# When a load may wait for two neighbouring slots, and the order of three VectorE instructions in the last MLP

## The chip, the cores and the metric

The kernel runs on one core of one Trainium2 chip. The metric is the device time of one execution in microseconds; the median of several runs counts. The core has a TensorE (matmul; its weight loads are shown as PEld), a VectorE (DVE), a ScalarE (ACT), a GpSimd (POOL) and a SyncE (SP), which issues all of this kernel's transfers from HBM on one queue served by 16 DMA engines.

## The reference

Two identical layers follow each other; each is an attention over a cache and then a small MLP mixer, for 8 batch rows with one token each (D = 448).

```python
def _A_ref(x, k_cache, v_cache, wq, wo):
    q = (x @ wq).reshape(B, Sq, 16, 256).transpose(0, 2, 1, 3)
    k = jnp.repeat(k_cache, 2, axis=1)          # k_cache, v_cache: (8, 8, 4096, 256) bf16
    v = jnp.repeat(v_cache, 2, axis=1)
    scores = jnp.einsum("bhqd,bhkd->bhqk", q, k) * (256 ** -0.5)
    p = _softmax(scores, axis=-1)
    o = jnp.einsum("bhqk,bhkd->bhqd", p, v)
    return o.transpose(0, 2, 1, 3).reshape(B, Sq, 4096) @ wo
...
    x = x + _A_ref(_layernorm(x), A_k_cache, A_v_cache, A_wq, A_wo)
    x = x + _B_ref(_layernorm(x), B_w1, B_w2, B_w3, B_w4)
    x = x + _A_ref(_layernorm(x), A_k_cache, A_v_cache, A_wq, A_wo)
    x = x + _B_ref(_layernorm(x), B_w1, B_w2, B_w3, B_w4)
```

With one token the shifts of `_B_ref` leave zeros, so that B reduces to `x + gelu(layernorm(x) @ w3) @ w4`. The two caches are 134 MB each. Both layers read the same K and V, and nearly all of the traffic is theirs.

## The kernel before

**Units.** The work is a list of 144 places, called units. A unit is (layer, batch row, K/V head), that is one head over 4096 positions, or a GAP, which is empty. A unit has four quarters; a quarter needs one part of K and one of V, each 512 KB. For each batch row b the list has layer 1's heads, then a short stretch of GAPs and one or two stray heads in which the MLP of layer 1 and the query projection of layer 2 run (`mid_steps`), then layer 2's heads. `ends` holds the unit of layer 1's last head of each row (9, 27, 45, 63, 81, 98, 115, 132). `fence` holds the first unit of layer 2 of each row (14, 32, 50, 68, 85, 102, 119, 136); it can't start before the query is there. "The gap" below is what lies between an end and its fence. Batch rows, or batches, are counted from 0.

**Slots.** 31 slots of 512 KB (`slab`, N_SLOTS) hold everything that is loaded. K goes through VectorE first (`transposes`, L554), from its raw slot into another slot, and is read by TensorE (L645, `k_part`). V is read by TensorE as it landed (L622, `v_part`). Layer 1's transposed K of six of the eight heads stays in its slots until layer 2 has read it; one of these heads has two of its quarters parked in PSUM, and ScalarE copies them back (L512, 1.0 us a copy). A slot goes to the list `free` when its last reader has been written down in the program, and `pump` is called.

**pump** (L502) takes the next part from `loads` while more than RESERVE = 1 slots are free. All of this happens when the program is built: it fixes which transfer is issued where in SP's queue and into which slot. On the chip each transfer then waits for the last reader of its slot. A part with an even number, whose neighbour is in `wide` and close in the list, may be loaded with that neighbour in one transfer of 1 MB, if two neighbouring slots are free (`take_two`). If none are and `under_way`, the parts that are loaded and not yet read, is at least ENOUGH = 7, pump returns and nothing is issued until the next slot comes free. If fewer are under way, the part is loaded alone, into the first slot that has no free neighbour (`take`). `wide` holds the parts that are used in "calm" units: those from one past a fence to the next end. Parts of the gap are always loaded alone.

**A unit's work** on the engines: scores on TensorE (L645), maxima on DVE and TensorE (L660, L668, L678), exponentials on ScalarE (L681), a turn on TensorE (L704) and four casts on ScalarE (L712) that make the weights `pt` for V, the sum (L719) and its reciprocal on GpSimd (L723). About six quarters later come V's matmuls (L622), and two scalings on ScalarE (L591, `head_out`) write the head's result. `wo_mms` (L180) multiplies it by wo.

**The end.** After the last unit the second layer's MLP runs for all rows at once (L832 to L909). VectorE makes the gelu in four steps around ScalarE's tanh (L872, L875, L878, tanh L879, L884). GpSimd makes two powers (L867, `rr[:, 1]` first, then `rr[:, 0]`). L880 and L883 add the normalised residual, which needs `rr[:, 0]`. L884 makes `hT`, the operand of the 56 matmuls with w4 (L891), and L898 adds their results to the residual, one quarter of the columns at a time.

Of the kernel before, what the change touches and what calls it, by code (L numbers as in the profile page):

```python
# [11 lines left out]
ALU = mybir.AluOpType  # L12
# [11 lines left out]
LAG = 6  # L24
ENOUGH = 7
PAIR_VIEW = 12


@with_exitstack
def kernel(  # L30
# [14 lines left out]
    nc = tc.nc  # L45
# [345 lines left out]
    n_units = len(units)  # L391
# [11 lines left out]
    t = 0  # L403
    while t < n_units:
# [5 lines left out]
        n = 1  # L410
# [31 lines left out]
    for t in order:  # L442
        for s in range(4):
            i = late_v.get((t, s), 4 * t + s + LAG)
            if t in ends or units[t + 1 : t + 2] == [GAP]:
                i = 4 * t + (6, 6, 7, 7)[s]
            elif t + 1 == n_units:
                i = 4 * t + (5, 5, 6, 7)[s]
# [3 lines left out]
    loads = []  # L452
    wide = set()
    calm = [any(f < t for f in [-1] + list(fence) if not any(f < e < t for e in ends)) for t in range(n_units + 2)]
    k = 0
    for i in range(4 * n_units + 8):
        n = len(loads)
        while k < by[min(i, 4 * n_units - 1)]:
            loads.append(("k",) + parts[k])
            k += 1  # L460
        loads += [("v",) + p for p in plan.get(i, [])]
        if calm[min(i // 4, n_units)]:
            wide.update(loads[n:])
        t, q = divmod(i + 2, 4)
        if t < n_units and units[t] and units[t][0] == 2 and (units[t][2], q) in parked:
            loads.append(("p", t, q))
# [3 lines left out]
    under_way = [0]  # L470

    def take():

        lone = [x for x in free if x ^ 1 not in free]
        x = min(lone or free)
        free.remove(x)
        return x

    def take_two():

        both = [x for x in free if x % 2 == 0 and x + 1 in free]
        if both:
            free.remove(both[0])
            free.remove(both[0] + 1)
        return both[:1]
# [16 lines left out]
    def pump():  # L502
        while loads and len(free) > RESERVE:
            kind, t, i = loads[-1]
            _, b, g = units[t]
            if kind == "p":
                loads.pop()
                x = take()
                dst = slots[x].rearrange("p (e q c x) -> p q c e x", e=4, q=2, c=4)
                for j in range(2):  # L510
                    src = park[parked[g, i]][j][:].bitcast(BF16)
                    nc.scalar.copy(dst[:, j], src.rearrange("p (c e x) -> p c e x", c=4, e=4))  # L512
                kt_of[(1, b, g), i] = x
                continue
            cache, of = (A_k_cache, raw_of) if kind == "k" else (A_v_cache, v_of)
            n, two = 1, (kind, t, i + 1)
            if i % 2 == 0 and two in wide and two in loads[-PAIR_VIEW:]:
                x = take_two() if len(free) > RESERVE + 1 else []
                if x:
                    n, x = 2, x[0]  # L520
                    loads.remove(two)
                elif under_way[0] >= ENOUGH:
                    return
            loads.pop()
            if n == 1:
                x = take()
            src = cache[b, g].rearrange("(p s e) d -> p s (e d)", s=4, e=8)
            nc.sync.dma_start(
                slab[:, UNIT * x : UNIT * (x + n)].rearrange("p (s d) -> p s d", s=n),
                src[:, i : i + n],  # L530
            )
            for m in range(n):
                of[t, i + m] = x + m
            under_way[0] += n
            n_loads[0] += n
            if n_loads[0] >= 8 and extra:
                nc.sync.dma_start(*extra.pop(0))
# [3 lines left out]
    def transposes(i):  # L541


        while len(parts) - len(todo) < by[i]:
            t, s = todo[-1]
            if 4 * t + s > i and ((t, s) not in raw_of or not free):
                return
            todo.pop()
            raw = raw_of.pop((t, s))
            kt = kt_of[units[t], s] = take()  # L550
            src = slots[raw].bitcast(FP32).rearrange("p (q c e i) -> p q c e i", q=2, c=4, e=4)
            dst = slots[kt].bitcast(FP32).rearrange("p (e q c r) -> p q c e r", e=4, q=2, c=4)
            for q in range(2):
                nc.vector.transpose(dst[:, q], src[:, q])  # L554
            _, b, g = units[t]
            if (g, s) in parked:
                for q in range(2):
                    dst = park[parked[g, s]][q][:].rearrange("p (c e r) -> p c e r", c=4, e=4)
                    nc.vector.transpose(dst, src[:, q])
            free.append(raw)  # L560
            under_way[0] -= 1
            pump()
# [49 lines left out]
    def v_part(t, s):  # L612
        if s == 0:
            at = PO + 4 * (nth[t] % n_po)
            pos[t] = pyb[:, at : at + 4].rearrange("p (k h) -> p k h", h=2)
            if nth[t] == n_po // 2:
                nc.vector.memset(pyb[:, PO : PO + 4 * (len(order) - n_po)], 0.0)
        v = v_of.pop((t, s))
        vv = slots[v].rearrange("p (c d) -> p c d", d=Dh)
        for c in range(8):  # L620
            for k in range(2):
                nc.tensor.matmul(  # L622
                    pos[t][:, k, :],
                    vv[:, c, 128 * k : 128 * k + 128],
                    pts[t][:, 8 * s + c, :],
                    start=(t == 0 and s == 0 and c == 0 and k == 0),
                    stop=True,
                    skip_group_check=True,
                )
        free.append(v)  # L630
        under_way[0] -= 1
        pump()

    def k_part(t, s):
        u = units[t]
        p, b, g = u
        if s == 0:
            assert t not in runs or t in ready
            scs[t] = scb[t % 2][:, 0:64].rearrange("p (c b h) -> p c b h", b=4, h=2)
        key = (u if fresh(u, s) else (1, b, g)), s  # L640
        ktv = slots[kt_of[key]].rearrange("p (e c m x) -> p e c m x", e=4, c=2, x=2)
        for c in range(2):
            for db in range(4):
                for x in range(2):
                    nc.tensor.matmul(  # L645
                        scs[t][:, 2 * s + c, :, :],
                        ktv[:, db, c, :, x],
                        Qblk[run_of[t][0]][:, run_of[t][1], db, x, :, :],
                        start=(db == 0 and x == 0),
                        stop=(db == 3 and x == 1),  # L650
                    )
        if p == 2 or g in loose or (g, s) in parked:
            free.append(kt_of.pop(key))
            pump()
# [80 lines left out]
    for t in rowst:  # L735
# [10 lines left out]
        out=xc, in0=xf, scalar1=st[:, 1:2], scalar2=None, op0=ALU.add  # L746
# [6 lines left out]
        out=st[:, 3:4], in0=st[:, 2:3], in1=mhalf[0:Bn, 0:1], op=ALU.pow  # L753
# [30 lines left out]
    for t in range(n_units + 1):  # L784
        cur = t < n_units
        for q in range(4):
            i = 4 * t + q
# [50 lines left out]
    u, hh = fd[:, 128 : 128 + HC * Bn], fd[:, 256 : 256 + HC * Bn]  # L838
    hT = slots[3][:, 0 : HC * Bn]
# [10 lines left out]
        out=cu, in0=xb2, in1=mu.unsqueeze(2).to_broadcast([128, Bn, 4]), op=ALU.add  # L850
# [11 lines left out]
    for i in (1, 0):  # L862
        f, e = TWICE[i]
        nc.vector.tensor_scalar(
            out=tt[:, i], in0=va, scalar1=-f, scalar2=e, op0=ALU.mult, op1=ALU.add
        )
        nc.gpsimd.tensor_tensor(  # L867
            out=rr[:, i], in0=tt[:, i], in1=mhalf[:, 0:1].to_broadcast([128, Bn]), op=ALU.pow
# [4 lines left out]
        out=hv, in0=hp.rearrange("p (m b) -> p m b", b=Bn), in1=r1, op=ALU.mult  # L873
    )
    nc.vector.scalar_tensor_tensor(  # L875
        out=u, in0=hh, scalar=0.044715, in1=hh, op0=ALU.mult, op1=ALU.mult
    )
    nc.vector.scalar_tensor_tensor(out=u, in0=u, scalar=1.0, in1=hh, op0=ALU.add, op1=ALU.mult)  # L878
    nc.scalar.activation(u, u, ACT.Tanh, scale=0.7978845608028654)  # L879
    nc.vector.tensor_tensor(  # L880
        out=sq, in0=cu, in1=rr[:, 0].unsqueeze(2).to_broadcast([128, Bn, 4]), op=ALU.mult
    )
    nc.vector.tensor_tensor(out=xb2, in0=xb2, in1=sq, op=ALU.add)  # L883
    nc.vector.scalar_tensor_tensor(out=hT, in0=u, scalar=1.0, in1=hh, op0=ALU.add, op1=ALU.mult)  # L884
    xo = slots[5][:, 64 : 64 + 4 * Bn].rearrange("p (b c) -> p b c", c=4)
    xoc = xo.rearrange("p b c -> p c b")
    opp = scb[1][0:Bn, 64:512]
    for c in range(4):
        yp = (scb[0] if c % 2 else dnb)[:, 32 * c : 32 * c + Bn]
        for m in range(HC):  # L890
# [8 lines left out]
            out=xoc[:, c], in0=yp, scalar=0.5, in1=Xc[:, c], op0=ALU.mult, op1=ALU.add  # L899
# [40 lines left out]
```

## Time and profile before

| | us |
|---|---|
| time, median of 3 runs (lowest, highest) | 1124.85 (1121.68, 1127.41) |
| the profiled execution's own time | 1124.39 |
| its span, from the first to the last instruction | 1122.6 |
| TensorE matmul busy | 684.8 (61%) |
| VectorE busy | 549.3 (49%) |
| ScalarE busy | 306.8 (27%) |
| read from HBM | 446.77 MB |
| transfers of V: 1 MB, 512 KB | 155, 202 |
| transfers of K: 1 MB, 512 KB | 109, 102 |

The profile cuts the span into 40 slices of 28 us. For each engine it gives the busy share in tenths, and for the 16 DMA engines the mean busy share and the GB/s moved. A DMA engine counts as busy while a packet is under way, also where that packet takes longer than its bytes need, so the rate tells more than the share. In lists of waits the name behind the arrow is what ended a wait: "<-DMA slab<-in_A_v_cache_dram" means that the engine stood until a transfer of V had landed, and "issue" is time in which the engine waited for nothing that the profile shows. The chain of waits is followed back from the last instruction; here it reaches back to 958 us.

### The profile page before, as it was taken

The numbers are of one execution on the slowest core, as the hardware profiler recorded it, in microseconds if no ns is written. First come the engines' busy times: TensorE is split into PE (matmuls) and PEld (weight loads), VectorE is DVE, ScalarE is ACT, GpSimd is POOL, SyncE is SP. The second block draws the span as 40 slices with busy tenths as digits, with TensorE's granted clock in tenths as the row PEclk, the third lists the DMA queues.
The fourth block names the chain that finished last, engine by engine and source line by source line (L and its number), as shares of the span: only waits on it lengthen the run. The fifth ranks groups of instructions, "written<-read, shape, count | busy, mean of one in ns | idle before, by whom it ended". The sixth has DMA issues, their size and how long they took to land. (4 is left out here: it accounts for less than half of the span.)

```text
span 1122.6 us, 46232 instructions
## 1 busy us (share of the span) xinstructions
PE 684.8 (61%) x20737; PEld 640.8 (57%) x20737; DVE 549.3 (49%) x1305; ACT 306.8 (27%) x1360; POOL 104.2 (9%) x156
## 2 busy tenths in 40 slices
PE   3345675666656575665756676666666665565765
PEld 2334564566646575655646565555656665565765
DVE  4347544644455445554546534653456425554322
ACT  1112223321332212421233222422243222421241
POOL 0000000100000000100001001000001000100101
DMA  9999999999999999999999999999999999999992
GB/s 366 396 419 425 405 409 424 423 418 389 392 425 423 411 402 420 424 423 395 418 403 424 412 412 388 425 423 413 363 417 424 422 402 374 424 422 411 363 403 93
DMA packets 89174, 449.76 MB, mean 401 GB/s; under 512 B 9344, under 2 KB 15376, under 8 KB 54800
## 3 DMA queue, kind: packets, MB, share of 16 engines
q1 hardware_dynamic: 88976, 446.81, 98.0%
q8 instruction: 162, 2.65, 0.8%
q14 instruction: 36, 0.29, 0.1%
HBM read 446.77 MB, written 0.01 MB: 398 GB/s over the span
## 5 line engine op out<-in xcount | busy, mean ns | idle before, releaser
L554 DVE STREAM_TRANSPOSE slab<-slab 128x512 f32<-128x512 f32 x640 | 413.4, 686 | 217.0 <-DMA slab<-in_A_k_cache_dram 158.1
L622 PEld LDWEIGHTS <-slab 128*128 128x128 bf16 x8192 | 273.5, 106 | 296.9 <-DMA slab<-in_A_v_cache_dram 245.5
L622 PE MATMUL bank<-pt,slab 128*128 128x2 bf16 x7168 | 259.9, 166 | 246.0 <-DMA slab<-in_A_v_cache_dram 174.7
L645 PE MATMUL bank<-Qblk,slab 128*128 128x8 bf16 x8192 | 296.9, 168 | 71.3 <-DVE slab L554 40.0
L645 PEld LDWEIGHTS <-slab 128*128 128x128 bf16 x8192 | 268.0, 105 | 78.7 <-DVE slab L554 47.4
L681 ACT ACTIVATE pe<-bank,small 128x32 bf16<-128x32 f32 x256 | 61.3, 296 | 417.1 <-DVE small L678 417.1
L723 POOL TENSOR_TENSOR small<-small 128x2 f32<-128x2 f32 x112 | 78.2, 698 | 794.1 <-DVE small L719 794.1
L712 ACT CAST pt<-bank 32x64 bf16<-32x64 f32 x448 | 91.1, 203 | 100.6 <-PE bank L704 96.1
L678 DVE TENSOR_REDUCE small<-bank 128x2 f32<-128x256 f32 x128 | 54.1, 423 | 103.3 <-PE bank L668 103.0
L719 DVE TENSOR_REDUCE small<-bank 128x2 f32<-128x64 f32 x128 | 27.2, 212 | 124.9 <-ACT pt L712 106.4
L164 ACT CAST Qblk<-bank 32x32 bf16<-32x32 f32 (+1 forms) x272 | 48.4, 178 | 121.2 <-PE bank L158 118.9
L668 PE MATMUL bank<-rows,small 128*128 128x128 bf16 x256 | 48.5, 293 | 19.0 <-DVE small L660 18.8
L660 DVE TENSOR_REDUCE small<-bank 128x2 bf16<-128x64 f32 x128 | 26.4, 206 | 59.6 <-PE bank L645 59.4
L622 PE MATMUL bank<-pt_far,slab 128*128 128x2 bf16 x1024 | 36.9, 166 | 25.0 <-DMA slab<-in_A_v_cache_dram 24.3
L704 PE MATMUL bank<-pe,rows 128*128 128x64 bf16 x512 | 51.2, 241 | 0.5 <-issue 0.5
L704 PEld LDWEIGHTS <-rows 128*128 128x128 bf16 x512 | 33.7, 124 | 27.8 <-issue 27.5
L694 PE MATMUL bank<-pe,small 128*128 128x64 bf16 x128 | 27.3, 213 | 33.4 <-ACT pe L681 32.0
L180 PEld LDWEIGHTS <-wo_sb 128*128 128x128 bf16 x1152 | 35.5, 104 | 8.6 <-issue 7.5
L180 PE MATMUL bank<-OT,wo_sb 128*128 128x1 bf16 x1024 | 33.2, 165 | 5.5 <-ACT OT L591 4.5
L135 PEld LDWEIGHTS <-wq_sb 128*128 128x128 bf16 x864 | 30.6, 106 | 9.2 <-issue 4.7
L512 ACT COPY slab<-park 128x1024 bf16<-128x1024 bf16 x32 | 30.4, 1024 | 8.2 <-DVE slab L554 6.1
L591 ACT ACTIVATE OT<-bank,small 128x2 bf16<-128x2 f32 x122 | 25.5, 261 | 23.9 <-PE bank L622 22.5
(113 smaller groups left out, 386.4 us busy)
## 6 DMA issues: line engine op xcount, KB each, us to landing
slab<-in_A_v_cache_dram SPq DMA_DIRECT2D x155, 1024.0 KB, 12.6
slab<-in_A_k_cache_dram SPq DMA_DIRECT2D x109, 1024.0 KB, 12.9
slab<-in_A_v_cache_dram SPq DMA_DIRECT2D x202, 512.0 KB, 8.0
slab<-in_A_k_cache_dram SPq DMA_DIRECT2D x102, 512.0 KB, 8.6
wo_sb<-in_A_wo_dram SPq DMA_DIRECT2D x4, 896.0 KB, 11.3
wq_sb<-in_A_wq_dram SPq DMA_DIRECT2D x3, 1024.0 KB, 6.8
w_sb<-in_B_w_dram SPq DMA_DIRECT2D x1, 1568.0 KB, 12.4
w_sb<-in_B_w_dram SPq DMA_DIRECT2D x3, 448.0 KB, 16.8
```

Source lines behind the costliest of these rows:

```text
L135: nc.tensor.matmul(pv[:, i, j, :], cols(big[:, c, :], m + i * half), rows[:, c, :], start=(i == 0 and j == 0 and c == 0), stop=True, skip_ ...
L164: nc.scalar.copy(dst, src)
L180: nc.tensor.matmul(y[:, c, :], chunk(wo_sb[:, k, :], c), o[:, k, :], start=False, stop=True, skip_group_check=True,)
L554: nc.vector.transpose(dst[:, q], src[:, q])
L622: nc.tensor.matmul(pos[t][:, k, :], vv[:, c, 128 * k : 128 * k + 128], pts[t][:, 8 * s + c, :], start=(t == 0 and s == 0 and c == 0 and k ...
L645: nc.tensor.matmul(scs[t][:, 2 * s + c, :, :], ktv[:, db, c, :, x], Qblk[run_of[t][0]][:, run_of[t][1], db, x, :, :], start=(db == 0 and x ...
L668: nc.tensor.matmul(mzs[t][:, 128 * h : 128 * h + 128], pm[:, h : h + 1].to_broadcast([128, 128]), ident, start=True, stop=True,)
L678: nc.vector.tensor_reduce(nm, mx, AX.X, ALU.max, negate=True)
L681: nc.scalar.activation(pe[:].rearrange("p c b h -> p h (c b)")[:, h], scs[t].rearrange("p c b h -> p h (c b)")[:, h], ACT.Exp, bias=nm[:, ...
L704: nc.tensor.matmul(pp[:, c], sel, pe[:], start=True, stop=True)
L712: nc.scalar.copy(pts[t][sl].rearrange("p (k c) h -> p k c h", c=4), pp[sl, :, :, pb, :].rearrange("p c k h -> p k c h"),)
L723: nc.gpsimd.tensor_tensor(out=rz_of[t], in0=zs, in1=mone, op=ALU.pow)
```

## The change

Two constants, SETTLE = 3 and BEFORE = 1, and a second set, `firm`, are added. A unit t is `at_ease` when units t - 3 to t are all calm, so from the fourth unit past a fence to the next end. Parts that are used then are in `firm`. Only for a pair whose second part is in `firm` does pump return to wait for two neighbouring slots; any other even part is loaded alone at once where no two neighbouring slots are free, whatever is under way. Which parts may form a pair (`wide`) stays as it was. Apart from that, L884 moves ahead of L880 and L883.

```diff
 PAIR_VIEW = 12
+SETTLE = 3
+BEFORE = 1
...
     calm = [any(f < t for f in [-1] + list(fence) if not any(f < e < t for e in ends)) for t in range(n_units + 2)]
+    firm = set()
+    at_ease = [all(calm[max(t - SETTLE, 0) : t + BEFORE]) for t in range(n_units + 1)]
...
         if calm[min(i // 4, n_units)]:
             wide.update(loads[n:])
+        if at_ease[min(i // 4, n_units)]:
+            firm.update(loads[n:])
...
                     loads.remove(two)
-                elif under_way[0] >= ENOUGH:
+                elif under_way[0] >= ENOUGH and two in firm:
                     return
...
     nc.scalar.activation(u, u, ACT.Tanh, scale=0.7978845608028654)
+    nc.vector.scalar_tensor_tensor(out=hT, in0=u, scalar=1.0, in1=hh, op0=ALU.add, op1=ALU.mult)
     nc.vector.tensor_tensor(
         out=sq, in0=cu, in1=rr[:, 0].unsqueeze(2).to_broadcast([128, Bn, 4]), op=ALU.mult
     )
     nc.vector.tensor_tensor(out=xb2, in0=xb2, in1=sq, op=ALU.add)
-    nc.vector.scalar_tensor_tensor(out=hT, in0=u, scalar=1.0, in1=hh, op0=ALU.add, op1=ALU.mult)
```

## The prediction

> **What bounds the kernel now.** I read the page's slices first, then the chain of waits, then windows, the SP queue and TensorE in time around a late fence, and the last 10 us. The page:
>
> ```profile
> DMA  9999999999999999999999999999999999999992
> GB/s 366 396 419 425 405 409 424 423 418 389 392 425 423 411 402 420 424 423 395 418 403 424 412 412 388 425 423 413 363 417 424 422 402 374 424 422 411 363 403 93
> DMA packets 89174, 449.76 MB, mean 401 GB/s; under 512 B 9344, under 2 KB 15376, under 8 KB 54800
> ```
>
> The DMA engines look busy in every slice, but the rate swings from 425 to 363 GB/s. The low slices recur once a batch, around the fence. The chain of waits shows who sets the pace between fences and at the end:
>
> ```profile
> 977.22 11.85 DMA slab<-in_A_v_cache_dram
> 990.74 14.14 DMA slab<-in_A_v_cache_dram
> 1032.87 4.68 DMA slab<-in_A_v_cache_dram
> ```
>
> Up to 1037 it is made of V transfers. After that, in the last batch, no DMA stands on it: only TensorE, DVE, ScalarE and "issue". So a microsecond saved in the queue before 1037 moves the end; one saved later does not. By windows (columns: busy times, granted clock, DMA share, GB/s):
>
> ```profile
> 960.00:1020.00 60.00, 38.14 (x1193) 36.36 (x1193) 34.47 (x73) 20.43 (x93) 6.63 (x10) 1.00 1.01 422
> 1031.00:1044.00 13.00, 10.15 (x314) 9.71 (x313) 4.94 (x24) 0.64 (x3) 0.69 (x1) 1.00 1.02 405
> 1044.00:1056.00 12.00, 9.88 (x315) 9.61 (x311) 4.47 (x16) 3.41 (x16) 1.24 (x2) 1.00 0.91 341
> 1056.00:1068.00 12.00, 8.30 (x259) 7.94 (x257) 4.03 (x11) 5.39 (x20) 1.41 (x2) 1.00 1.02 357
> ```
>
> Pairs give 422, singles in a full queue 405, and around the fence (unit 136, 1051.2) 341 and 357: the queue runs dry. The SP queue shows how:
>
> ```profile
> 1053.62 2.85 SPq L528 DMA_DIRECT2D slab<-in_A_v_cache_dram  x3
> 1057.66 0.33 SPq L528 DMA_DIRECT2D slab<-in_A_k_cache_dram  x1
> 1063.38 2.33 SPq L528 DMA_DIRECT2D slab<-in_A_v_cache_dram  x2
> ```
>
> Nothing is issued from 1058.0 to 1063.4. Replaying the bookkeeping of pump with the kernel's own rules, up to eight slots are free then and no two of them are a pair.
>
> **The change, first part.** Building both programs gives 568 cache transfers before (264 pairs, 304 singles) and 605 after (227 and 378): 37 pairs are split. TensorE's and GpSimd's instructions keep their order.
>
> *Cost.* In the trace's packet records a 4 KB packet took 159 ns, an 8 KB one 309 ns, a semaphore packet 9 ns; each of 16 engines moves eight packets. A single is 8 x 159 + 9 = 1281 ns, a pair 8 x 309 + 9 = 2481 ns, so a split costs 2 x 1281 - 2481 = 81 ns. Landings agree: 1.24 apart for queued singles, 2.43 for pairs. 35 splits lie before the last fence: +2.8 us. Two lie behind it, off the chain. The 37 more issues take SP 0.33 us each (12 us if nothing covered them), in stretches where SP waits for slots anyway.
>
> The Trainium skill ("DMA: Bandwidth & Descriptors", "Rules for kernel authors") asks for at least 1 MiB a DMA, which speaks against this part. The rows above, 405 against 422 GB/s, agree in direction but make the loss about 3%.
>
> *Gain.* No row shows the changed queue, so I laid both lists of transfers over the trace of before: a transfer issues 0.35 us after the last reader of its slot has ended (the median of all issues); it lands 1.29 us (single) or 2.50 us (pair) after the one ahead, the fetches' share included, or, if the queue was dry, 4.5 us plus its own time after issue (such issues at 690.2, 801.7 and 1063.7 show 4.6 to 4.9, one at 1049.6 shows 2.7). Time in which the queue is dry, before and after, by batch from 0: 0 and 0, 0.8 and 0, 0.5 and 0.9, 0.5 and 0.2, 1.6 and 0, 3.0 and 2.4, 3.0 and 2.1: 9.4 against 5.5 us, a gain of 3.9 (with 2.7 for the start, 2.4 against 0.9). I take 4.5, which three of four rows show and which lands before's own transfers within 1.5 us of where they landed. The last batch goes from 3.6 to 0, which the chain doesn't see.
>
> Of the 5.5 left, 3.8 is a new place: three units past the fence pairs are waited for again, and slots that singles broke up have no pair. That price holds if slots are read as late as before. TensorE past the fence waits for V, though, so earlier V frees slots earlier:
>
> ```profile
> 693.31 0.58 PE L622 MATMUL bank<-pt,slab 128*128 128x2 bf16 x16 [2.47 <-DMA slab<-in_A_v_cache_dram]
> 697.98 0.58 PE L622 MATMUL bank<-pt,slab 128*128 128x2 bf16 x16 [2.57 <-DMA slab<-in_A_v_cache_dram]
> 702.84 0.59 PE L622 MATMUL bank<-pt,slab 128*128 128x2 bf16 x16 [2.73 <-DMA slab<-in_A_v_cache_dram]
> 1072.52 0.19 PE L622 MATMUL bank<-pt,slab 128*128 128x2 bf16 x2 [2.79 <-issue]
> ```
>
> How much earlier is bounded by the last batch, where no V is waited for: its four units from the fence on take 23.9 us, batches 5 and 6 take 24.6 and 26.8. So their reads can come at most 0.7 and 2.9 earlier. That removes 0.7 of batch 5's 1.8, all 1.6 of batch 6's and, by estimate, 0.3 of batch 2's 0.4. Left are 2.9, the gain is 6.5. Bounds: no gain, if all the dry time moves; and 10, if all 3.8 vanish (7.7) and so does the dry time that my laying-out misses. Landings spaced wider than their bytes sum to 14.0 us in the gaps and first units of batches 0 to 6, less 2.7 for instruction fetches (162 packets of 0.94 us on 16 engines are 0.85% of the time) 11.4, so 2.0 are missed.
>
> *What moves with it.* The four copies of parked K (0.94 us each on ScalarE) are issued from pump and move. In batch 3 they go behind the head's L591, in 6 behind L712 and L591, so TensorE's waits for L591 there (4.21 and 6.47) shrink by up to 3.7; in 4 and 5 they go behind L712 but stay ahead of L591, which then ends up to 0.85 later (the four casts). DMA was never dry at those places, so I take 0; without that cover, -7.4 to +1.7. In the last batch two of the four move ahead of L681 into an idle 2.05 us of ScalarE: 0.
>
> *Last batch.* TensorE stops there inside groups of matmuls for "issue", each time beside one 16 KB instruction packet. With nine to twelve half-megabytes outstanding such stops last 2.85, 2.01, 1.18 and 1.90, with seven or fewer 0.88 to 1.07. Two of the latter (1058.7, 1064.5) will see a fuller queue: 0 to +2.0; I take +0.5, as the queue at the second is nearly as full as at stops near 1.0.
>
> **Second part**, the tail:
>
> ```profile
> 1113.56 3.24 POOL L867 TENSOR_TENSOR slab<-slab,small 128x8 f32<-128x8 f32 x2 [5.97 <-DVE slab L864]
> 1116.15 0.30 ACT L879 ACTIVATE slab<-slab 128x112 f32<-128x112 f32 x1 [6.44 <-DVE slab L878]
> 1116.83 0.19 DVE L880 TENSOR_TENSOR slab<-slab 128x32 f32<-128x32 f32 x1 [0.71 <-POOL slab L867]
> 1117.17 0.27 DVE L884 SCALAR_TENSOR_TENSOR slab<-slab 128x112 bf16<-128x112 f32 x1
> 1117.48 1.67 PE L891 MATMUL bank<-slab,w_sb 128*128 128x8 bf16 x56 [2.90 <-DVE slab L884]
> ```
>
> The tanh ends at 1116.45, but L884 stands behind L880, which waits for GpSimd's second power until 1116.80. Moved ahead it starts 0.08 after the tanh (as L719 after L712 at 1106.43), at 1116.53 instead of 1117.17: -0.65. The residual then ends at 1117.25, hidden under the first fourteen of 56 matmuls (to about 1117.40); 0.15 us of cover.
>
> **Sum** against the profiled execution's own 1124.39 us (span 1122.6 and 1.8 around it): +2.8 - 6.5 + 0.5 - 0.65 = -3.85, **1120.5 us**. That execution lies 0.46 under the median of 1124.85, which I leave.
>
> **Rivals.**
> *The queue never dries.* Gain 10: +2.8 - 10 + 0.5 - 0.65 = -7.35, 1117.0. For it: V is waited for after each of the first seven fences. Against: slots in the gap come free at the pace of the chain through the MLP.
> *The wait only moves.* Reads come no earlier, gain 3.9, both late stops lengthen by half their bound (+1.0): -0.75, 1123.6. For it: batch 5's four units have 0.7 to give.
> *Slower: instruction fetches take the place of V waits.* Past each fence the queue is fuller, and each stop of TensorE grows from 1.0 to 2.0. Fetches start about 6 us apart, four in four units. In batches 0 to 6 this eats all that the earlier V gives (gain 0), in the last it adds 4 x 1.0: +2.8 + 4.0 - 0.65 = +6.15, 1130.5. It decides from about 0.6 us a fetch. Against it: at 680.8, 808.7 and 927.0 stops of 1.9 to 2.45 came with only four or five outstanding. The Trainium skill ("DMA: Bandwidth & Descriptors", "Queues, rings and completion order") has each DMA engine alternate between queues packet by packet, by which depth would not matter and this rival falls; the stops of the last batch don't fit that.
> *Each transfer pays its start.* If the start of each added transfer is not covered, 37 x 2.7 (the shortest dry start) is +100, 1224. The landings 1.24 apart speak against it.
> That the change does nothing is ruled out by the 37 splits in the built program.
>
> **Chances and range.** Forecast 0.42 (own range 1118 to 1123.5), queue never dry 0.28, wait moves 0.17, fetches 0.11, starts 0.02. The range 1114 to 1128 takes in the first three with the spread of the runs (1121.7 to 1127.4) and leaves out the last two and about 0.05 below. About 0.5%, 5.6 us, can be told from no change: faster (under 1119.2) is 0.28 plus 0.13 of the forecast's 0.42, 0.41; slower 0.11 + 0.02 = 0.13; the rest 0.46.
>
> **What would show it.** SP issues singles in the first three units past each fence, with no silence of 3 us or more there; the rate in the window at the last fence rises from 341 and 357 towards 400; V waits of TensorE past fences 4 to 6 shrink; the drained stretch, if it moves, stands three units past fences 5 and 6; the last operand (now L884) starts within 0.1 us of the tanh's end. I am wrong if the queue stays wet and the time does not fall (TensorE or its fetches set the pace), or if the rate between fences falls from 422.

## The result and the profile after

| | before | after |
|---|---|---|
| median of 6 runs each, us (lowest, highest) | 1122.87 (1121.43, 1127.41) | 1116.01 (1115.19, 1120.21) |
| ratio, 95% interval | | 0.9939 [0.9916, 0.9963] |
| profiled execution, us (its span) | 1124.39 (1122.6) | 1116.44 (1114.6) |

The change makes the kernel 6.9 us faster (4.2 to 9.4). The forecast was 1120.5, with 1118 to 1123.5 as its own range; the rival "the queue never dries", 1117.0, came nearest. The page of the kernel after, its slices of 28 us:

```profile
GB/s 364 393 417 425 401 417 423 424 418 395 417 423 424 402 401 419 422 424 390 414 420 424 400 410 416 421 423 412 395 419 425 407 411 397 422 422 405 384 413 101
```

The high slices are as high as before (425). The low ones around the fences have risen: apart from the first slice, and the last two in which the loads end, the lowest is 384 where it was 363. Windows over the four units that begin at the fences of batches 4, 5 and 6 show it closer (columns: stretch, its length, busy times of five engines, granted clock, DMA share, GB/s). Before:

```profile
677.90:704.20 26.30, 14.69 (x478) 14.02 (x476) 15.05 (x30) 6.31 (x31) 2.10 (x3) 1.00 0.99 386
803.60:828.20 24.60, 14.98 (x476) 14.05 (x476) 14.92 (x30) 6.34 (x31) 2.10 (x3) 1.00 0.98 379
926.50:953.30 26.80, 14.97 (x478) 14.16 (x476) 15.08 (x30) 6.28 (x31) 2.10 (x3) 1.00 0.98 372
```

After:

```profile
678.50:700.30 21.80, 14.95 (x478) 14.40 (x476) 12.72 (x27) 6.44 (x31) 2.10 (x3) 1.00 1.03 418
801.90:823.50 21.60, 14.83 (x475) 14.22 (x474) 11.01 (x24) 6.39 (x31) 2.10 (x3) 1.00 1.02 413
922.80:946.20 23.40, 15.31 (x481) 14.62 (x479) 12.99 (x27) 6.44 (x31) 2.10 (x3) 1.00 1.01 397
```

TensorE does the same work (some 15 us of matmuls) in 3.0 to 4.5 us less, and the queue moves 397 to 418 GB/s. Of the waits of TensorE in the third stretch (engine, line, what it waited for: total us, times, longest), before:

```profile
PE bank L622 <- DMA slab<-in_A_v_cache_dram: 6.4, 3, 2.8
PE bank L645 <- issue: 3.0, 2, 1.8
```

After:

```profile
PE bank L628 <- issue: 3.2, 2, 1.7
PE bank L651 <- issue: 2.7, 2, 1.8
...
PE bank L628 <- DMA slab<-in_A_v_cache_dram: 0.7, 1, 0.7
```

V waits went from 7.8, 4.6 and 6.4 to 0.9, 0.8 and 0.7 us in the three stretches, 16.4 in all. The stretches are 10.9 shorter. The rest went into "issue", of which there were 2.4, 3.8 and 3.0 us and now are 3.6, 5.9 and 5.9, 6.2 more in all.

The SP queue in the middle one of these stretches (start, length, engine and line, what it moves, how many issues). Before, around the fence:

```profile
802.70 0.38 SPq L528 DMA_DIRECT2D slab<-in_A_k_cache_dram  x1
806.64 0.80 SPq L528 DMA_DIRECT2D slab<-in_A_v_cache_dram  x2
810.06 0.33 SPq L528 DMA_DIRECT2D slab<-in_A_k_cache_dram  x1
```

After, later in the stretch:

```profile
811.75 3.08 SPq L534 DMA_DIRECT2D slab<-in_A_v_cache_dram  x2
816.90 0.33 SPq L534 DMA_DIRECT2D slab<-in_A_k_cache_dram  x1
821.84 1.97 SPq L534 DMA_DIRECT2D slab<-in_A_v_cache_dram  x2
```

From 817.23 to 821.84, three units past the fence, SP issues nothing: the wait for pairs is still there and has moved, as the prediction laid it out. But it does no harm. What SP had issued less what the packets of its queue had moved, counted from the same traces, in transfers of 512 KB:

| batch 5 | SP silent, us | outstanding at its start | at its end |
|---|---|---|---|
| before | 803.1 to 806.6 | 3.6 | 1.7 |
| before | 807.5 to 810.1 | 3.1 | 1.4 |
| after | 817.2 to 821.8 | 6.9 | 3.3 |

The pause of the kernel after is longer than either of the two before, but it starts with twice as much in the queue and ends with more left in it.

Past the last fence the rates rise less. Windows of the kernel after, placed 5 us earlier than those of the prediction since its last fence comes 5.2 us earlier:

```profile
955.00:1015.00 60.00, 37.35 (x1155) 34.82 (x1153) 33.95 (x71) 18.29 (x85) 6.29 (x9) 1.00 1.01 419
1026.00:1039.00 13.00, 9.29 (x288) 8.90 (x285) 5.16 (x24) 0.64 (x3) 0.70 (x1) 1.00 1.02 416
1039.00:1051.00 12.00, 9.79 (x306) 9.53 (x304) 4.55 (x14) 3.85 (x18) 1.25 (x2) 1.00 0.99 374
1051.00:1063.00 12.00, 9.04 (x278) 8.57 (x278) 4.15 (x10) 7.32 (x23) 1.41 (x2) 1.00 0.98 362
```

374 and 362 GB/s, where 341 and 357 were; ahead of them 419 and 416, where 422 and 405 were. Past this fence SP is silent from 1049.7 to 1055.2, with 5.5 transfers outstanding at the start and 1.7 at the end. Even so, the time from the last fence to the end of the span went from 71.4 to 68.6 us, and only 0.6 of these 2.8 us are the tail. TensorE's idle time put down to "issue" fell there from 11.8 to 8.7 us: eight stops of 0.8 us or more became five.

The tail (the timeline of the kernel after):

```profile
1106.09 3.24 POOL L873 TENSOR_TENSOR slab<-slab,small 128x8 f32<-128x8 f32 x2 [5.98 <-DVE slab L870]
1108.69 0.30 ACT L885 ACTIVATE slab<-slab 128x112 f32<-128x112 f32 x1 [6.45 <-DVE slab L884]
1109.02 0.28 DVE L886 SCALAR_TENSOR_TENSOR slab<-slab 128x112 bf16<-128x112 f32 x1 [0.36 <-ACT slab L885]
```

The operand (now L886) starts at 1109.02, 0.03 us after the tanh ends, and no longer waits for GpSimd's pair of powers, which ends at 1109.33.

### The profile page after: what moved, and what is told of

Read it like the earlier page. It is cut to its first block, busy times and chain, and to the rows that moved or that the text cites. A ratio compares the mean times of both kernels' runs of the same rounds, so it can differ in the third digit from the quotient of the medians.

```text
span 1114.6 us, 46349 instructions
## 1 busy us (share of the span) xinstructions
PE 686.8 (62%) x20737; PEld 640.3 (57%) x20737; DVE 550.7 (49%) x1305; ACT 307.2 (28%) x1360; POOL 104.4 (9%) x156
## 4 chain that ended last, share of the span: by engine, by line
DMA 39%; PE 15%; ACT 6%; issue 5%; DVE 5%; POOL 0%; SPq 0%; DVEq 0%; ACTq 0%; POOLq 0%
DMA slab<-in_A_v_cache_dram 31%; DMA slab<-in_A_k_cache_dram 8%; PE bank L628 5%; PE bank L651 3%; DVE slab L560 3%; ACT pt L718 2%; PE bank L137 2%; ACT slab L518 1%; ACT pe L687 1%; DVE small L684 1%; PE bank L674 1%; PE bank L710 1%; ACT pt_far L718 1%; PE bank L700 1%; PE bank L313 1%
## 5 line engine op out<-in xcount | busy, mean ns | idle before, releaser
L674 PE MATMUL bank<-rows,small 128*128 128x128 bf16 x256 | 48.5, 293 | 10.9 <-DVE small L666 10.9
L137 PE MATMUL bank<-small,wq_sb 128*128 128x1 bf16 x768 | 28.1, 165 | 6.0 <-issue 6.0
```

The costliest lines, as they stand in the source:

```text
L137: nc.tensor.matmul(pv[:, i, j, :], cols(big[:, c, :], m + i * half), rows[:, c, :], start=(i == 0 and j == 0 and c == 0), stop=True, skip_ ...
L674: nc.tensor.matmul(mzs[t][:, 128 * h : 128 * h + 128], pm[:, h : h + 1].to_broadcast([128, 128]), ident, start=True, stop=True,)
```

## The experiments

All ratios are against the kernel before, run beside it. The runs of one group share these (17, 15 and 25 of them in the three groups). In microseconds a result is its ratio, less 1, times their median. The ratio is not the quotient of the two medians, so the difference of the medians can lie up to 0.8 us away from it.

### Which part, and which fence

**The queue without the moved operand.** The three VectorE instructions stand in the old order.

```diff
-    nc.vector.scalar_tensor_tensor(out=hT, in0=u, scalar=1.0, in1=hh, op0=ALU.add, op1=ALU.mult)
     nc.vector.tensor_tensor(
...
     nc.vector.tensor_tensor(out=xb2, in0=xb2, in1=sq, op=ALU.add)
+    nc.vector.scalar_tensor_tensor(out=hT, in0=u, scalar=1.0, in1=hh, op0=ALU.add, op1=ALU.mult)
```

> The changed queue without the moved operand of the last MLP. My theory (time saved in the dry queue before the last fence is worth its own length, the tail 0.6 us): 1116.6, 0.6 above the changed kernel, ratio to before 0.9945. Rival (the whole gain is in the last batch and the tail): no different in this run, it is told by the next two.

Measured: 1116.83 against 1123.89, 0.9931 [0.9918, 0.9943], so -7.8 us. The first part makes the whole gain that runs can tell.

**The wait dropped past the last fence alone**, the operand moved.

```diff
-                elif under_way[0] >= ENOUGH and two in firm:
+                elif under_way[0] >= ENOUGH and (two in firm or len(loads) > 50):
```

> Moved operand as in the change; the waits for pairs go only past the last fence (2 pairs split in place of 37), the seven fences before it wait as before. My theory (past the last fence TensorE's own chain sets the pace, no transfer stands on it): only the tail's 0.6 us, 1122.3, ratio 0.9994 and not under 0.998. Rival (the last batch gives a good part, as its TensorE wait for V also falls): 1119 to 1120, ratio 0.997.

Measured: 0.9987 [0.9976, 0.9997], -1.5 us (0.3 to 2.7), of which some 0.6 is the moved operand. In its profiled execution 69.1 us lie between the last fence and the end.

**The wait dropped at the first seven fences alone**, the operand moved.

```diff
-                elif under_way[0] >= ENOUGH and two in firm:
+                elif under_way[0] >= ENOUGH and (two in firm or len(loads) <= 50):
```

> Moved operand as in the change; the waits for pairs go past the first seven fences, the last one waits as before (34 pairs split). My theory: all of the gain, 1116 to 1117, ratio 0.994. Rival (the last batch gives a good part): 1119 to 1120, ratio 0.997.

Measured: 1116.89, 0.9931 [0.9918, 0.9944], the same as the queue part at all eight. The gain comes from the missing waits at the first seven fences; what the last adds lies below what these runs can tell. In this run too the stretch behind the last fence is shorter than before, 68.6 against 71.4 us, though its waits are those of before (the moved operand alone has 71.2). So part of what the first seven fences give seems to be cashed only behind the last one; these are single executions.

**The moved operand alone**, in the kernel before.

> The moved operand alone, queue as before. Theory: in the profile the operand of w4 starts within 0.1 us of the tanh's end, and from the last V matmul to the end of the span 12.9 us as in the changed kernel, against 13.5 before; a time 0.6 us lower can't be told from one run. Rival (the residual behind it delays the adds of the results): 13.3 or more.

One run, 1123.69. Its time says nothing at this size; the tail of its trace does:

```profile
1116.05 0.30 ACT L879 ACTIVATE slab<-slab 128x112 f32<-128x112 f32 x1 [6.44 <-DVE slab L878]
1116.38 0.28 DVE L880 SCALAR_TENSOR_TENSOR slab<-slab 128x112 bf16<-128x112 f32 x1 [0.36 <-ACT slab L879]
```

The operand follows the tanh by 0.03 us here too. From the last unit's last V weight load to the end of the span it is 12.83 us, against 13.50 before and 12.94 after: -0.67 and -0.56 us.

### What a split costs, and what a wait costs

**Every pair in two halves**, issued one after the other into the same slots, in the kernel before: 264 splits and no other slot, wait or order.

```diff
-            nc.sync.dma_start(
-                slab[:, UNIT * x : UNIT * (x + n)].rearrange("p (s d) -> p s d", s=n),
-                src[:, i : i + n],
-            )
+            for m in range(n):
+                nc.sync.dma_start(slots[x + m], src[:, i + m])
```

> Before, with each of its 264 transfers of 1 MB issued as two of 512 KB, one right after the other, into the same slots at the same place in the queue: 832 transfers, all waits as they were. Theory (a split costs 81 ns of transfer time and no more): 257 of them before the last fence, +20 to +21 us, 1143.5, ratio 1.018. Rival 1 (each transfer pays a start that is not covered): +2.7 us each and more, over 1800. Rival 2 (a split costs nothing where the queue is full): 1123, ratio 1.000.

Measured: 1135.14 against 1125.38, 1.0092 [1.0078, 1.0105], +10.4 us by the ratio. That is half of the 20 to 21 that 81 ns a split asks for. In the trace of before 250 of the pairs, not 257, are issued ahead of the last fence; 10.4 over these is 41 ns.

**No wait anywhere**: 817 transfers and 15 pairs, so 249 pairs given up.

```diff
-                elif under_way[0] >= ENOUGH and two in firm:
+                elif False:
```

> The changed kernel without any wait for two neighbouring slots, calm stretches too: 817 transfers, 15 pairs. Theory: 249 splits of 81 ns before the last fence are +20, the dry time of the first seven batches (about 10) goes, the tail 0.6: 1122.9 + 20 - 10 - 0.6 = 1132, ratio 1.008. Rival (splits are free, waits are all the cost): 1113 or less, ratio 0.991. Rival (slots, not waits, keep the queue dry, so waits gave little): 1138 or more, ratio 1.014.

Measured: 1.0016 [1.0006, 1.0025], +1.8 us. The forecast of 1.008 missed, since its price of a split was too high. 235 of the splits lie ahead of the last fence: +19.0 at 81 ns, +9.6 to +11.3 at 41 to 48 (48 is the price of the halves elsewhere, below). What comes back is then 8 to 9.5 us, the tail's 0.6 among it.

**The wait from 10 under way on, instead of 7**, in the kernel before (83 pairs given up).

```diff
-ENOUGH = 7
+ENOUGH = 10
```

> Before, with ENOUGH at 10 in place of 7 and nothing else changed: a pair is waited for everywhere in the calm stretches, but only with ten parts under way. 651 transfers, 83 pairs split. Theory (what counts is that no wait lets the queue run dry, however that is reached): 83 x 0.081 = 6.7 less some 10 of dry time: 1119.5, ratio 0.997, 3 to 4 us above the changed kernel without its tail. Rival (waits past the fence cost for another reason than depth, place alone counts): 1127 or more, ratio 1.004.

Measured: 1119.54, 0.9949 [0.9936, 0.9963], -5.7 us, where 0.997 was expected. Another rule for when to wait, without the change's units and fences, brings most of the gain. Its windows past the same three fences show why:

```profile
679.50:702.20 22.70, 14.60 (x478) 14.16 (x476) 11.11 (x25) 6.34 (x31) 2.10 (x3) 1.00 1.02 417
803.00:825.30 22.30, 14.83 (x476) 14.11 (x476) 11.15 (x24) 6.34 (x31) 2.10 (x3) 1.00 1.01 403
925.80:948.40 22.60, 15.30 (x478) 14.30 (x476) 12.52 (x27) 6.43 (x31) 2.10 (x3) 1.00 1.01 400
```

The units are about as short and the rates about as high as in the kernel after.

**The copies of parked K behind all else of their step**, in the kernel after.

```diff
-                    nc.scalar.copy(dst[:, j], src.rearrange("p (c e x) -> p c e x", c=4, e=4))
+                    backs.append((dst[:, j], src.rearrange("p (c e x) -> p c e x", c=4, e=4)))
...
+            while backs:
+                nc.scalar.copy(*backs.pop(0))
```

> The changed kernel with ScalarE's copies of parked K always behind the casts and the head's scaling of their quarter, in all eight batches. Theory (earlier reads of slots at the fourth unit come from V landing earlier; the copies stand where the queue is full): no change from the changed kernel, 1116, ratio to before 0.994. Rival (the gain above my forecast comes from the copies that the change moved): another 3 us or more, 1113, ratio 0.991.

Measured: 0.9934 [0.9921, 0.9946], nothing that differs from the change. Where these copies stand on ScalarE makes no difference that the runs can tell.

### Whether it is the pieces or the waiting

After the second group two readings were left: that smaller pieces help by themselves around a fence, since their first half lands and frees its slot sooner, or that only the missing wait does.

**Halves around the fences**, in the kernel before: the 31 pairs that are not in `firm` (built as in the change) go as two transfers into the pair's slots, and the wait for the pair stays.

```diff
-            nc.sync.dma_start(
...
+            if n == 2 and two not in firm:
+                for m in range(n):
+                    nc.sync.dma_start(slots[x + m], src[:, i + m])
+            else:
+                nc.sync.dma_start(
...
```

> Before, with only the 31 pairs that are used up to three units past a fence issued as two halves, one right after the other, into the same slots, all waits as before. New theory, from the halves of all pairs costing 9.8 us and not 20 (a split past the fence takes its 81 ns out of time in which the queue would be dry anyway, and its first half lands 1.2 us earlier, so slots come free earlier): 0 to -3 us, ratio 0.997 to 1.000. Old theory (81 ns each wherever): +2.5, ratio 1.002.

Measured: 1127.34 against 1124.36, 1.0019 [1.0003, 1.0035], +2.1 us. Halves alone bring no gain, so the theory that had them bring up to 3 us falls. 31 splits are +2.5 at 81 ns and +1.4 at 45: this run can't tell the two prices apart.

**Halves everywhere else**: the same edit with `two in firm`, 233 pairs.

> Before, with the other 233 pairs (used from four units past a fence to the next end) issued as two halves, waits as before. New theory (there the queue is full and each split pays): with the 31 past the fence costing nothing or less, the 9.8 of all halves are paid here, +10 to +13, ratio 1.009 to 1.012. Old theory (81 ns each): +18.9, ratio 1.017.

Measured: 1.0094 [1.0071, 1.0117], +10.6 us. Over the 221 of these pairs that are issued ahead of the last fence this is 48 ns a split (36 to 60 by the interval; 81 ns for all 233 would be +18.9). A window of a steady stretch gives the loss directly. Before, in pairs:

```profile
710.00:760.00 50.00, 32.17 (x995) 30.47 (x996) 29.50 (x62) 16.34 (x77) 5.58 (x8) 1.00 1.01 424
```

In halves:

```profile
715.00:765.00 50.00, 32.92 (x997) 30.71 (x997) 29.56 (x62) 16.52 (x77) 5.59 (x8) 1.00 1.03 417
```

424 against 417 GB/s: the 1.7% more time of a pair's 2.48 us is 42 ns.

**Waiting again from the second unit past a fence** (247 pairs, so 17 given up), the rest as in the kernel after.

```diff
-SETTLE = 3
+SETTLE = 1
```

> The changed kernel with SETTLE at 1: pairs are waited for again from two units past a fence on (17 pairs split in place of 37). Theory (each unit past the fence without a wait fills the queue a little more): about half of the gain, 1120, ratio 0.997. Rival (the first unit is all that counts): as the change, ratio 0.993 to 0.994.

Measured: 1126.46, 1.0018 [1.0003, 1.0033], +2.0 us, slower than before. Both theories are wrong here: one expected half of the gain, the other all of it. The windows past its three fences:

```profile
679.40:704.00 24.60, 14.94 (x478) 14.18 (x476) 14.96 (x30) 6.43 (x31) 2.11 (x3) 1.00 0.99 365
805.50:829.90 24.40, 15.17 (x476) 14.21 (x476) 14.86 (x30) 6.38 (x31) 2.10 (x3) 1.00 0.95 358
930.30:955.80 25.50, 15.16 (x481) 14.33 (x479) 15.17 (x30) 6.37 (x31) 2.10 (x3) 1.00 0.97 377
```

358 to 377 GB/s, no better than the 372 to 386 of before. Its SP queue in batch 5:

```profile
802.97 1.47 SPq L534 DMA_DIRECT2D slab<-in_A_k_cache_dram  x1
808.59 1.15 SPq L534 DMA_DIRECT2D slab<-in_A_v_cache_dram  x2
```

SP is silent for 4.2 us from 804.4, with 3.4 transfers outstanding, and 0.3 when it ends; and again from 813.7 to 816.8, from 3.8 down to 1.4. The stop here is no longer than the one of the kernel after (4.6 us). It comes earlier, and meets a queue of 3.4 transfers in place of 6.9. That the queue decides and not the place is what the wait from 10 under way shows.

**Waiting again only from the sixth unit** (193 pairs).

```diff
-SETTLE = 3
+SETTLE = 5
```

> The changed kernel with SETTLE at 5: two more units without a wait (71 pairs split). Theory (at the fourth and fifth unit the queue of the changed kernel is wet although SP stands still for some 5 us there, so nothing is left to gain and 34 more splits pay 81 ns): +2.8 against the change, 1119, ratio 0.996. Rival (the wait that moved to the fourth unit costs what my forecast gave it): 1113 to 1114, ratio 0.991.

Measured: 1119.56, 0.9957 [0.994, 0.9973], -4.8 us (3.0 to 6.8), as the theory had it. Dropping more waits than the change does brings nothing more; 34 more splits at 45 ns would be +1.5, which the intervals can't tell from nothing. No kernel tried is clearly faster than the change.

### The account of the queue

From the packet records of each trace, as in the prediction: a stretch of time less its packets' own times (159, 309, 9 ns and 936 for an instruction packet, on 16 engines). The sum runs from the first gap to the last fence: eight gaps, and what lies between for batches 0 to 6. Below nothing means that packets moved faster than these times add up to. Time in us:

| kernel | pairs given up | gap | fence and four units | rest | sum | ratio |
|---|---|---|---|---|---|---|
| before | 0 | 5.9 | 9.0 | -2.1 | 12.8 | 1 |
| after | 37 | 5.5 | -2.1 | -0.2 | 3.2 | 0.9939 |
| again from the second unit | 17 | 4.3 | 10.0 | -1.0 | 13.3 | 1.0018 |
| again from the sixth unit | 71 | 6.8 | -0.8 | -2.1 | 3.9 | 0.9957 |
| wait from 10 under way | 83 | 6.6 | -1.6 | -4.2 | 0.8 | 0.9949 |
| never waits | 249 | 4.8 | 1.2 | -8.9 | -2.9 | 1.0016 |
| halves everywhere | 264 | 4.4 | 9.2 | -9.0 | 4.6 | 1.0092 |
| halves around the fences | 31 | 9.5 | 8.7 | -2.2 | 16.0 | 1.0019 |
| halves elsewhere | 233 | 3.7 | 9.6 | -8.4 | 4.9 | 1.0094 |

Each row is one execution. A second one with the queue of before (the moved operand alone) sums to 12.0, and the queue without the moved operand to 3.8, so differences under 1 us say little. Two things stand in the table. The column of the fence is 8.7 to 10.0 in every kernel that waits in the first three units past the fence from seven parts under way on, whether its pieces are pairs or halves, and -2.1 to 1.2 in the others. And the rest is far below nothing where many pairs are split, down to -9.0, because two halves take less time than their packets' own times say: the split is cheaper than 81 ns.

## Why the prediction came out as it did

The time lies in the range, 4.5 us below the forecast and below the forecast's own range. 1.5 of the 4.5 is the starting point: the forecast starts from 1124.39, and the kernel before had 1122.87 in the runs beside the change. The gain was 6.9 us where 3.85 were forecast. The mechanism was right, the sizes of its terms were not, and most of the error was in the one that was worked out at the greatest length.

**What bounds the kernel** (right up to the last fence). Microseconds saved in the queue at the first seven fences moved the end: in the two profiled executions the last row's last unit of layer 1 comes 6.2 us earlier, its fence 5.2 and the end 8.0. The 2.8 us between the fence and the end are more than the tail's 0.6, so "one saved later does not" goes too far, or the stops there got shorter for a reason of their own.

**Cost of a split, 81 ns, +2.8** (mis-sized). Measured 41 to 48 ns, so 35 splits are about +1.6. The step that failed is the sum of packet durations, and "Landings agree" was a misreading: twice 1.24 less 2.43 is 50 ns, not 81. The landings were in hand and gave nearly the measured price. The Trainium skill ("DMA: Bandwidth & Descriptors", "Rules for kernel authors") asks for 1 MiB at least; its direction is confirmed, with 424 against 417 GB/s, but in a full queue it is worth under 2%, not the 4% of 405 against 422 (which the prediction put at about 3%). The matching window of the kernel after has 416, in singles too, so the 405 was not the price of singles alone.

**Dry queue, 9.4 to 2.9, -6.5** (mis-sized; the bound of 10 was near). In the same currency the account gives 12.8 to 3.2, so -9.6; with splits at their measured price, which the packets' own times overstate by 1.2 us in all, some -8.4. Two of its steps failed:
- "Of the 5.5 left, 3.8 is a new place." The pause three units past the fence is where it was said to be (817.2 to 821.8), but it was priced with the reads of the trace before. By the time it comes the queue holds 6.9 transfers, where the first stops at the fences before met 3.1 to 4.6 in batches 4 to 6. The run that waits again from the second unit shows the price when the queue has had no time to fill: all of the gain.
- "So their reads can come at most 0.7 and 2.9 earlier." The last batch's 23.9 us was taken as TensorE's own pace. It is no floor: the four units take 21.8, 21.6 and 23.4 us now in batches 4 to 6, and the last batch's own four went to 22.5. That no V is waited for there did not make it one: its queue stood dry too (341 GB/s), and "issue" stops of 4.5 us in these four units (2.3 now) were taken for TensorE's pace.

The dry time in the gaps (5.9 to 5.5) stayed, as the argument against the rival said; that rival had its size from the right total, though not because the queue never dries.

**Moved copies of parked K, 0** (right), shown by the run that puts them last.

**Fetch stops in the last batch, +0.5** (the wrong way). Behind the last fence TensorE had eight "issue" stops of 0.8 us or more before, 11.4 us in all, and has five now, 8.4 in all, each beside an instruction packet; the last two before, at 1095.3 and 1101.2, have no counterpart. This is one execution of each kernel, and no run shows what sets these stops; it does not bear out a rule by which a fuller queue lengthens them. The slower rival falls by the time, but it had something. Past the fences of batches 4 to 6 "issue" took 6.2 of the 16.4 us that V waits lost. The stops are no longer than before (the longest 2.4, 1.8 and 1.8 us against 2.4, 2.3 and 1.8); there are ten of them instead of six. So they were not made longer by the fuller queue, as the rival had it; that the added ones had been hidden under V waits fits, since four instruction packets before (at 692.4, 702.2, 826.3 and 951.9) start inside a wait for V, two in the kernel after; but no run shows it. The prediction gave this no term outside the last batch.

**Tail, -0.65** (right): -0.56 to -0.67 by the traces.

The sum with measured sizes is 1.6 - 8.4 - 0.6 = -7.4, against -6.9 (-4.2 to -9.4) by the runs. That it comes so near is partly luck. In the profiled executions the last fence came 5.2 us earlier, not 6.8: of the difference 0.8 is data that had been moved ahead by then (0.65 of a half-megabyte), 0.5 lies ahead of the first gap. The last batch gave some 2.2, for which the sum has no term. The rival "the queue never dries" came nearest with a cost that was too high (2.8 for 1.6) and a gain that was too high (10 for 8.4), which offset each other. "Each transfer pays its start" is excluded by the halves at 41 to 48 ns each.

**Of the signs named in advance**, the V waits, the place of the moved pause (batch 5) and the operand came as said. The rate between the fences falls little (419 against 422, with 16 pairs and 11 singles in the window where there were 20 and 6). Past the fence of batch 4 one silence of 3.6 us, with 6.2 transfers outstanding at its start, already falls into the third unit. Two did not: at the last fence the rate stayed at 374 and 362, not "towards 400", and SP is silent there for 5.5 us, since parts used from the fourth unit on are asked for early in that batch and wait for a pair. That is off the chain: the run with the first seven fences alone is as fast.

**What stays open**: how much the last fence gives (0 to about 2 us), why the stretch behind it is some 2 us shorter even where its waits stay, and why two halves in a row move some 2% faster than their packets' durations add up to.

## What to carry to other kernels

A rule that holds a transfer back for a better shape has to be judged by what is in the queue when it holds: here a pause of 4.6 us cost nothing that a run could show with seven half-megabytes outstanding, and one of 4.2 us drained the queue with three. Price a change in transfer size from the spacing of landings in a full queue, or from a run that splits all transfers into the same slots, not from sums of packet durations. And a stretch of the same kernel is no floor for another as long as its own supply runs dry: here it got shorter itself.

## What the hardware did that was not expected

Halving a transfer of 1 MB costs 41 to 48 ns in a full queue here, though its packets' durations say 81. And stopping a little earlier made it worse than no change at all: waiting again from the second unit instead of the fourth turned a gain of 6.9 us into a loss of 2, with pauses of SP no longer than 4.6 us in batches 4 to 6, as in the kernel after, but with emptier queues at their start.
